# A gated linear attention with an MoE behind it, one core: transposes of k ahead of the products, all products of a chunk in one piece, and the first tile in four parts

## The chip, the cores and the metric

The kernel runs on one core of one Trainium2 chip. The metric is the device time of one execution in microseconds; 715.45 us is the median of three runs of the kernel before (712.55 to 721.03).

## The reference

For 4 batches x 8 heads, a sequence of 768 steps with head size 48 goes through a complex diagonal recurrence; the result goes through a gated two-layer product (384 to 2048 to 384).

```python
mag = np.sqrt(a_re * a_re + a_im * a_im)
scale = np.minimum(mag, 0.999) / (mag + 1e-06)
a_re_n, a_im_n = (a_re * scale, a_im * scale)
for t in range(S):
    ar, ai = (a_re_n[:, :, t, :, None], a_im_n[:, :, t, :, None])
    new_re = ar * S_re - ai * S_im
    new_im = ar * S_im + ai * S_re
    kv = np.einsum('bhd,bhe->bhde', k[:, :, t], v[:, :, t])
    S_re, S_im = (new_re + kv, new_im)
    y[:, :, t] = np.einsum('bhd,bhde->bhe', q[:, :, t], S_re)
...
h = x @ w_in
g = h * np.clip(h + 3.0, 0.0, 6.0) / 6.0
return (g @ w_out).astype(np.float32)
```

## The kernel before

The sequence is cut into 24 chunks of 128 steps (6 for each batch; the chunks of two batches alternate, so chunk `cc` hands its state to chunk `cc+2`). Three chunks make a tile of `a` (`z`, 8 tiles, two in memory at a time) and also a group of MoE (8 groups of 384 rows). The work is written as thirteen generators, called streams. One string, `ORDER`, names the stream whose next step is issued; a step runs to the next `yield`. Nothing is reordered afterwards: each engine, and SyncE (SP) with its DMAs, takes its instructions in the order in which the steps were issued and waits in that order. Some letters of the string:

- `Z` (`load`, line 344): a DMA of one part of a tile of `a`. `PARTS` (line 79) cuts a tile in two, one for each half `f` of the steps, 9 rows each.
- `N`, `O` (`normal`, line 361): the parts with even and with odd number are brought to the reference's magnitude, in four steps: Square on ScalarE (ACT, line 373), a product on POOL, or on VectorE (DVE) for tile 0 (376), Ln and Exp (377, 381, 382), a product (383), then three or four DVE products (385 to 393). Two buffers `sq` serve all parts.
- `C` (`chain`, line 398): cumulative products over the 64 steps of a half: seven steps of four DVE operations (408 to 410), four smaller ones, and a last step (437 to 451) that multiplies all 18 rows at once, six DVE operations of 882 elements with a temporary `fx`. Then POOL works out the decay of the state between chunks (455 to 475) and six DMAs lay it out as `cw` (482).
- `P`, `Q` (`prep`, line 493; `Q` is chunk 1 alone): q and k of a chunk, multiplied with the chain's result, and laid out by six DMAs as `kq` (543); one DMA brings `vt` (551).
- `A` (`mat`, line 556), the attention of one chunk on TensorE (PE): scores `pA` from `kq`, masked by DVE into `am` (570); products of v into `py` (578 to 597); if there is a chunk behind it, k is transposed into `pt` and copied by ACT to `kn`, which takes `am`'s buffer (599 to 604); if there is one before it, the state decays (POOL 612, DVE 618) and its products are added into `py` (620 to 627); `pG` updates the state (632 to 639); ACT and DVE split `py` into `xh` and `xl` for MoE (647, 648). The PSUM pool `ps_a` has three buffers for `pA`, `py`, `pt` and `pG`.
- `M` (`moe`, line 652): for each of 16 blocks `f` of the hidden size nine products into `ph` (690), the gate (ACT 696, DVE 699 or 708, called `hs` below), and the products of the block before into `po` (673 to 677). Groups 0 to 2 have three `po` products for a block, groups 3 to 7 nine.
- `D`, `W` load and convert the 16 weight blocks (DVE 308, 312, ACT 307, 316, POOL 317); `G` and `S` look at the weights' ranges and split them; `V` ends it.

```python
        py = ps_a.tile([C, 3, C], F32, tag="ps", name="py")
...
        if has_g:
            kn = pe_.tile([C, NH, L], F32, tag="am", name="kn", bufs=1)
```

Of the kernel before, what the change touches and what calls it, by code (L numbers as in the profile page):

```python
# [35 lines left out]
ORDER = (
    "ZNNZZZONQNOOOCNCCCCOCCCCCCOCCPDWPODDDWPQPPPPPPWWQWQWDQQQQPOANAPPWDAAACDWAAWWAAWNWNWPDDDWWPZPCWWCNAZA"
    "APDDWCWAAADACOAAACAACCACAMMCWMMMDCMMMMMCCCMMMWPMMMMMMMMMMMMPWPPMMMMMMMMWMDMMCMMWPPWMMMMMOWWPPMMMMMMM"
    "NMMMMOMWWMMMMDMMMAMMAMMPPMMMMANAAAPWPPMMPWNWMMMOPPPAAMMMMMMMMMMMMACPCMMMPGCPCGPGGGCCCCCMCMMMMMMMMPAA"
    "MGGZZCCCPAAAACOMMMMMMMMPPPMAAAMMMMMPPNAAAPPAPAAANMONAAPOMPMNMMMMMMOPMAAPMGMMMMMCMMMMPMMGPMMGGAAAACCC"  # L40
    "MMCPCMMMMMCCCGAMMMGMMMMPPPPGGAPPPMSSCAMMMMMMMAMMAMMMMGMMMMCCPCMGMAAPAAMMPPPPMMMMMMGMAMGMMMPMZZAAMMMM"
    "MMCNNPPAMAMMOMNMMAPOPMPMMMMMOMNOAMAMMMMMMPMMMMGMMMMMMMMMMAGAPCMMMMMPPCPAAAMMACMMMAACAACCCCMMGPMMMMMA"
    "MMPPPMMGGPGAMPPCCCMMMMMMMMMMMZAMAMASSCCNMMMMMMGNMMMPSMMPPSMMAPMMMMMPMASMSMMZGNSMPMMMMPPMMOMNAMSSMMMM"
    "MMPAASSSAOPMMMMMMAASPMMMMMPPMSAPAAAGPPPPPSMMMOMMOCMMMMMMMMMACCMMSSSSAMMMSSSMMMMMMCMPPMMMMGMCAMMPCPSG"
    "GAPMMCAMAMMAMMMZCPMCMMMMMCCPPPAAAMAACNNMMMMMMMMSMMMMMMMAAMMMMMMCCMMMMZPAMMMMMMMMMMMAMMMMAMMMMAMSPPMP"
    "MPOMMMSAAAMMMMPMPMMSMMMCMMMMMMMMOMMMMMMMMPPOANAMMSSMMMMMMMPMMPPMPPAOAAMMMAMSMMMMMMMMMAMNMMMMMPPMMMCA"
    "MPCMMMMAAACCMMMMMMMMMMMPMMMAPAAMMMMMMPMMMAMMMMCMMMMMMMMMMMMZCMMMMMMMMPCMCMNPCCMMMMMMMNMMAAAAMMMMAMPC"
    "MMMMMMZMAAAAMNCMCMMMPMMMMAMAPMMMMMMMCMPMMMMPPPPMMMMMAMMMMMMMMMMMMMMNOMOMMMPMMMMMAPAPMMMMMMMMAMMAMMMM"
    "MOMAMMPAMPAOPPPPPMMMMMMMMMAMMMMCCMMMMMPCCMMMMMMMAMAAMMMMMMMMMMMPPCMMMMMPPMMMMACAAAMMMCMMMMMCMAMMMMMM"
    "PMMMCCAAMAMCMMMMMMMMMGMAMMMPMAAACACPCMAPAMMMMPMMMMMMMMPPMPPMMMMMMMMMMMMMMMMMMMMMPAPMMMMMMMMAAMPPMMMM"  # L50
    "MMMMMMMMMMMMMAAMAMAMMMMMPMPPPMMMMMMMMMMMMMMMMMMMMMMMMMMMAMAPPPMMMMMMMMMMMMPMMMMMMMMMMMMMMMMPAAMMPMPM"
    "MAMMMMMMMMMMMMMMMPMMAAAMMMMMMMMMPAAAMMMMMMMMMMMMMMMMMAAMMMAAMMMMMMMMMMMMMMMMMMMMMMMMMMMMMMMMMMMMMMMM"
    "MMMMMMMMMMMMMMMMMMMMMVMMMMMMMMMMMMMMMMMMMMMMMMMMMMMMMMMMMMMMMMMMMMMMMMMMMMMMMMMMMMMMMMMMMMMMMMMMMVMM"
    "MM"
)
# [175 lines left out]
def tile_gated_attention_moe(ctx, tc, aL, GL, vL, wL, maskL, qkvaL, out):  # L231
    nc = tc.nc
    V, A, P, T, SP = nc.vector, nc.scalar, nc.gpsimd, nc.tensor, nc.sync
# [322 lines left out]
    def mat(cc):  # L556
        g, c = GROUP[cc]
        while cc not in KQ:
            yield "wait"
# [37 lines left out]
        yield
        if has_g:
            kn = pe_.tile([C, NH, L], F32, tag="am", name="kn", bufs=1)
            for hf in range(2):  # L600
                pt = ps_a.tile([C, 4, L], F32, tag="ps", name="pt")
                for i in range(4):
                    T.transpose(pt[:, i], kt[:, hf * 4 + i], ident[:L, :L])
                A.activation(kn[:, hf * 4 : hf * 4 + 4], pt, AF.Copy)  # L604
                if hf and not has_s:
                    free("kq")
                yield
        if has_s:
            q, c2 = CHUNK[cc]
            while q not in CWs:  # L610
# [1 line left out]
            P.tensor_tensor(
                state2,
                state2,
                CWs[q][:, :, :, c2].rearrange("p h k -> p k h").unsqueeze(3).to_broadcast([L, 2, NH, 64]),
                ALU.mult,
            )
            V.tensor_tensor(xs, xs, xj, ALU.add)
            yield
        if has_s:  # L620
# [287 lines left out]
```

## Time and profile before

| | us |
|---|---|
| runs of the kernel before | 712.55, 715.45, 721.03 |
| the profiled execution | 718.27 |
| its span, from the first to the last instruction | 716.5 |
| PE busy, DVE busy, ACT busy, POOL busy in the span | 593.6, 510.7, 352.5, 175.9 |
| mean granted clock of PE | 0.975 of full speed |

A row of a timeline gives start and length in us, engine, line of the kernel, operation, written tile <- read tiles, shape and count; what stands in brackets is the engine's idle time before it and what ended that. A row of SPq is a DMA's issue on SyncE's queue, not its transfer. A shape is partitions x elements of one partition.

### The profile page before, as it was taken

The page shows a single profiled execution, that of the slowest core. Times are in us where ns is not written, and L with a number is a line of the kernel's source. Part 1 is how long each engine was busy: PE and PEld are TensorE (multiplying, and loading weights), DVE is VectorE, ACT ScalarE, POOL GpSimd, SP SyncE. Part 2 cuts the span into 40 slices and gives each one's busy share as a digit, 9 for nine tenths or more (in the row PEclk, how much of TensorE's full clock was granted, in tenths as well). Part 3 has the DMA queues.
Part 4 walks back from the last instruction along what each step waited for, and adds up shares of the span by engine and source line. Part 5 has one row for each costly group of instructions (what it writes and reads, how often), then busy time and mean ns, then how long its engine had stood idle before and what let it go on. Part 6 is the DMA issues. An engine that isn't in the chain of part 4 may idle for free.

```text
span 716.5 us, 12111 instructions
## 1 busy us (share of the span) xinstructions
PE 593.6 (83%) x4433; PEld 521.7 (73%) x4433; DVE 510.7 (71%) x995; ACT 352.5 (49%) x721; POOL 175.9 (25%) x193
## 2 busy tenths in 40 slices
PE   0005359998568989989998999999999999999995
PEld 0004347776356767777777999999999998998995
DVE  3998857989858876787888657987688855453432
ACT  5334332565657776567646454444643443423332
POOL 0204230342143143315740333221302211300000
PEclk9999999999689999999999999999999999999998
DMA  9009872257746885476566234242453244140001
GB/s 344 23 18 206 253 211 78 67 121 163 183 102 161 194 225 96 127 179 157 104 126 150 80 72 79 86 70 90 82 126 45 82 82 78 50 60 34 1 0 38
DMA packets 55508, 79.61 MB, mean 111 GB/s; under 512 B 12432, under 2 KB 40208, under 8 KB 55440
## 3 DMA queue, kind: packets, MB, share of 16 engines
q1 hardware_dynamic: 55440, 78.75, 46.7%
q8 instruction: 37, 0.61, 0.4%
q14 instruction: 31, 0.25, 0.1%
HBM read 51.05 MB, written 4.72 MB: 78 GB/s over the span
## 4 chain that ended last, share of the span: by engine, by line
PE 38%; DMA 9%; DVE 8%; ACT 7%; issue 3%; POOL 3%; SPq 1%; ACTq 0%; DVEq 0%; POOLq 0%
PE ph L690 15%; PE po L673 5%; PE po L674 5%; PE po L675 5%; DMA kq<-gg 3%; PE py L585 3%; DMA out_dram<-ot 2%; DMA wgs<-in_wL_dram 2%; PE pA L569 2%; PE po L677 2%; PE pG L632 1%; ACT r L696 1%; DVE gg L528 1%; POOL gg L518 1%; DVE pr L408 1%
## 5 line engine op out<-in xcount | busy, mean ns | idle before, releaser
L696 ACT ACTIVATE r<-ph,half 128x384 f32<-128x384 f32 x128 | 73.7, 577 | 113.9 <-PE ph L690 109.4
L677 PE MATMUL po<-wo,hs 128*128 128x384 f32 x288 | 108.3, 509 | 16.7 <-DVE hs L708 16.7
L690 PE MATMUL ph<-xh,win_l 128*128 128x384 f32 x384 | 102.7, 376 | 2.8 <-ACT xh L647 2.8
L569 PE MATMUL pA<-kq 96*128 96x128 f32 x384 | 53.9, 296 | 61.2 <-DMA kq<-gg 59.3
L569 PEld LDWEIGHTS pA<-kq 96*128 96x128 f32 x384 | 51.7, 209 | 63.8 <-issue 61.4
L690 PE MATMUL ph<-xl,win_h 128*128 128x384 f32 x384 | 90.5, 344 | 1.0 <-DVE xl L648 1.0
L690 PE MATMUL ph<-xh,win_h 128*128 128x384 f32 x384 | 89.9, 342 | 0.0
L699 DVE SCALAR_TENSOR_TENSOR ph<-r,ph 128x384 f32<-128x384 f32 x80 | 44.8, 560 | 62.5 <-ACT r L696 62.3
L673 PE MATMUL po<-wh,gl 128*128 128x384 f32 x240 | 84.9, 354 | 4.2 <-DVE gl L704 3.8
L677 PEld LDWEIGHTS po<-wo,hs 128*128 128x128 f32 x288 | 53.9, 197 | 44.6 <-DVE hs L708 18.5
L674 PE MATMUL po<-wout_l,gh 128*128 128x384 f32 x240 | 81.9, 341 | 0.0
L675 PE MATMUL po<-wh,gh 128*128 128x384 f32 x240 | 81.0, 337 | 0.0
L690 PEld LDWEIGHTS ph<-xh,win_l 128*128 128x128 f32 x384 | 70.4, 192 | 14.4 <-ACT xh L647 2.9
L704 DVE TENSOR_TENSOR gl<-ph,gh 128x384 fp32r<-128x384 f32 x80 | 44.5, 557 | 41.0 <-ACT gh L702 40.9
L690 PEld LDWEIGHTS ph<-xl,win_h 128*128 128x128 f32 x384 | 69.4, 191 | 1.9 <-DVE xl L648 1.5
L690 PEld LDWEIGHTS ph<-xh,win_h 128*128 128x128 f32 x384 | 69.5, 190 | 0.6 <-issue 0.6
L702 ACT ACTIVATE gh<-ph 128x384 fp32r<-128x384 f32 x80 | 39.2, 490 | 60.9 <-DVE ph L699 60.9
L408 DVE TENSOR_TENSOR pr<-z 128x288 f32<-128x288 f32 (+2 forms) x176 | 66.6, 419 | 1.4
L518 POOL TENSOR_TENSOR gg<-gg,u 128x384 f32<-128x384 f32 x18 | 19.5, 1084 | 142.4 <-ACT u L516 126.7
L632 PE MATMUL pG<-vt,kn 128*96 128x64 f32 x320 | 34.9, 268 | 21.4 <-ACT kn L604 21.4
L673 PEld LDWEIGHTS po<-wh,gl 128*128 128x128 f32 x240 | 45.5, 189 | 8.4 <-DVE gl L704 7.3
L632 PEld LDWEIGHTS pG<-vt,kn 128*96 128x96 f32 x320 | 33.3, 183 | 24.6 <-ACT kn L604 22.1
(101 smaller groups left out, 1042.9 us busy)
## 6 DMA issues: line engine op xcount, KB each, us to landing
kq<-gg SPq DMA_DIRECT2D x138, 128.0 KB, 4.7
ws<-in_wL_dram SPq DMA_DIRECT2D x16, 768.0 KB, 7.2
wgs<-in_wL_dram SPq DMA_DIRECT2D x32, 384.0 KB, 3.8
z<-in_aL_dram SPq DMA_DIRECT2D x16, 612.0 KB, 5.5
vt<-in_vL_dram SPq DMA_DIRECT2D x24, 256.0 KB, 5.2
out_dram<-ot SPq DMA_DIRECT2D x24, 192.0 KB, 1.9
u<-in_GL_dram SPq DMA_DIRECT2D x23, 192.0 KB, 5.0
gg<-in_GL_dram SPq DMA_DIRECT2D x23, 192.0 KB, 2.6
```

The source lines that it names most:

```text
L408: V.tensor_tensor(pr[:, j], src, fac[:, j : j + 1].to_broadcast([C, *shape]), ALU.mult)
L569: T.matmul(pA[:, i], kt[:, hf * 4 + i], qt[:, hf * 4 + i], start=True, stop=True)
L632: T.matmul(pG[:, n], kn[:, n], vt[:, n], start=True, stop=True)
L673: T.matmul(po[i], gl[:, ts], wout_h[f], start=f == 0, stop=False)
L674: T.matmul(po[i], gh[:, ts], LATE["wl"][:, f], start=False, stop=False)
L675: T.matmul(po[i], gh[:, ts], wout_h[f], start=False, stop=f == NFF - 1)
L677: T.matmul(po[i], hs[0][:, ts], wout[f], start=f == 0, stop=f == NFF - 1)
L690: T.matmul(ph, w[:, f, kt * C : (kt + 1) * C], xx[:, kt], start=k == 0, stop=k == 8)
L696: A.activation(r, ph, AF.Relu, scale=1.0 / 6.0, bias=half)
L699: V.scalar_tensor_tensor(ph, r, 1.0, ph, ALU.min, ALU.mult)
L702: A.activation(gh, ph, AF.Copy)
L704: V.tensor_tensor(gl, ph, gh, ALU.subtract)
```

## The change

1. In `mat` the transposes of k into `pt` and the copy to `kn` stand right behind the scores, and the decay of the state behind them. All products into `py`, those of v and those of the state, are issued in one step after that. A chunk with a chunk before it takes one step of `A` less (196 steps become 176).
2. `kn` is now `kk`, with a buffer of its own.
3. The last step of `chain` goes by 9 rows in place of 18: twelve operations of 441 elements in place of six of 882 (112 steps of `C` become 136); `fx` shrinks with it.
4. Tile 0 of `a` is cut in four parts (5 and 4 rows for each half); the other tiles stay at two.
5. `ORDER` is another one throughout. The first two hundred letters or so and the stretch around chain 2 are shown.

```diff
-    GS=3, VTB=2, IL=2
+    GS=3, VTB=2, IL=2, R0=5
...
-    "ZNNZZZONQNOOOCNCCCCOCCCCCCOCCPDWPODDDWPQPPPPPPWWQWQWDQQQQPOANAPPWDAAACDWAAWWAAWNWNWPDDDWWPZPCWWCNAZA"
-    "APDDWCWAAADACOAAAACAACCACAMMCWMMMDCMMMMMCCCMMMWPMMMMMMMMMMMMPWPPMMMMMMMMWMDMMCMMWPPWMMMMMOWWPPMMMMMMM"
-    "NMMMMOMWWMMMMDMMMAMMAMMPPMMMMANAAAPWPPMMPWNWMMMOPPPAAMMMMMMMMMMMMACPCMMMPGCPCGPGGGCCCCCMCMMMMMMMMPAA"
-    "MGGZZCCCPAAAACOMMMMMMMMPPPMAAAMMMMMPPNAAAPPAPAAANMONAAPOMPMNMMMMMMOPMAAPMGMMMMMCMMMMPMMGPMMGGAAAACCC"
...
+    "ZZNNOZZZNDNONQDDOONOZNNDOOOCCCCCOCCCCCCCCCCCWPPCPQPPPPPPWQWOQNQDQQWWAANPNWPWAAAPWDQAAPWWZNWOWOAZOAPC"
+    "CDDDWCWCCWCNAAPDDPPWAAAADAAACAWCAWAACWCWMMMMMMMMCCWCMMMMWMMMMCMWCWMCMMMMPPDMMMMMMMDMPDPPWPPMCMMMMMMM"
+    "MWWPNMMMMDMWWWMMMMMMMMMMMMAAMPNAAAPMMPPNMMMMWMMMPPMMMMMOAPOMMWMMPMMOAAAMMMMCPCPMCMMGMMMMCMMGAGCPACGP"
+    "CCAMMMGCPACCCCCCCMGGMMMMMMMZMPPMZMMAAAPMMMMPMPPNMMMNPONAAAPAAOPPMPMNAAAPOMMMMMMOMMMMMAGGGPCCPPCCMMMM"
...
 PARTS = [
-    [(f, x, min(9, 3 * n - x)) for f in range(2) for x in range(0, 3 * n, 9)] for _, n, _ in CHAINS
+    [(f, x, min(r, 3 * n - x)) for f in range(2) for x in range(0, 3 * n, r)]
+    for t, n, _ in CHAINS
+    for r in [9 if t else R0]
 ]
...
-        for x in range(0, w, 18):
-            xn = min(18, w - x)
+        for x in range(0, w, 9):
+            xn = min(9, w - x)
...
-        while cc not in VT:
-            yield "wait"
-        vt = VT.pop(cc)
-
-        py = ps_a.tile([C, 3, C], F32, tag="ps", name="py")
...
-        for n in range(NH):
-            ymm(n, False, vt, am[:, n], n < 4, False)
-        for k in range(2):
-            for n in range(k, NH, 2):
-                ymm(n, True, vt, am[:, n], False, k == 1 and not has_s)
-        if not has_g:
-            free("vt")
-        yield
         if has_g:
-            kn = pe_.tile([C, NH, L], F32, tag="am", name="kn", bufs=1)
+            kn = pe_.tile([C, NH, L], F32, tag="kk", name="kk", bufs=1)
...
             V.tensor_tensor(xs, xs, xj, ALU.add)
             yield
+        while cc not in VT:
+            yield "wait"
+        vt = VT.pop(cc)
+
+        py = ps_a.tile([C, 3, C], F32, tag="ps", name="py")
...
+        for n in range(NH):
+            ymm(n, False, vt, am[:, n], n < 4, False)
+        for k in range(2):
+            for n in range(k, NH, 2):
+                ymm(n, True, vt, am[:, n], False, k == 1 and not has_s)
+        if not has_g:
+            free("vt")
         if has_s:
-            sp = xs
             for n in range(NH):
-                ymm(n, False, sp, qt[:, n], False, False)
+                ymm(n, False, xs, qt[:, n], False, False)
             for k in range(2):
                 for n in range(k, NH, 2):
-                    ymm(n, True, sp, qt[:, n], False, k == 1)
+                    ymm(n, True, xs, qt[:, n], False, k == 1)
             free("kq")
-            yield
+        yield
```

## Rows read from the trace of the kernel before

**Rows 1.** Windows by stage: stretch, its length, busy us and instructions, PE clock, DMA.

```profile
0.00:117.61 117.61, 36.01 (x260) 30.67 (x261) 88.75 (x175) 45.83 (x78) 25.77 (x36) 1.00 0.57 163
117.61:221.24 103.63, 83.13 (x559) 64.64 (x559) 84.90 (x151) 56.73 (x117) 31.14 (x34) 0.90 0.56 132
221.24:716.50 495.26, 474.44 (x3617) 426.38 (x3615) 337.00 (x670) 249.97 (x527) 118.99 (x124) 0.98 0.43 95
...
5.60:20.34 14.74, 0.00 (x0) 0.00 (x0) 8.68 (x12) 9.53 (x16) 1.00 (x1) 1.00 0.93 368
...
167.90:186.06 18.16, 8.68 (x46) 7.00 (x44) 16.69 (x55) 12.27 (x31) 0.93 (x4) 0.80 0.65 173
...
176.70:186.70 10.00, 0.03 (x1) 0.04 (x1) 8.74 (x33) 6.99 (x17) 1.23 (x7) 0.60 0.72 170
186.70:218.00 31.30, 22.93 (x220) 16.86 (x220) 19.27 (x25) 18.02 (x38) 11.02 (x9) 0.80 0.61 137
...
396.00:702.00 306.00, 301.61 (x2362) 289.64 (x2361) 194.90 (x381) 129.50 (x262) 56.93 (x64) 1.00 0.31 64
```

(The busy times stand in the order PE, PE's weight loads, DVE, ACT, POOL.)

**Rows 2.** Waits of PE, 0 to 108 us and 108 to 216: total, times, longest.

```profile
PE pA L569 <- DMA kq<-gg: 59.3, 1, 59.3
PE pG L632 <- ACT kn L604: 18.6, 1, 18.6
...
PE po L677 <- DVE hs L708: 12.3, 4, 10.1
PE py L585 <- DVE am L570: 5.4, 1, 5.4
```

**Rows 3.** Timeline of the first tile and the start of chain 0.

```profile
5.61 1.16 ACT L373 ACTIVATE sq<-z 128x1152 f32<-128x1152 f32 x1 [3.59 <-DMA z<-in_aL_dram]
...
19.34 2.21 POOL L376 TENSOR_TENSOR sq<-sq 128x576 f32<-128x576 f32 x1 [18.35 <-ACT sq L373]
20.34 1.90 DVE L408 TENSOR_TENSOR pr<-z 128x288 f32<-128x288 f32 x2
...
22.27 0.31 DVE L409 TENSOR_TENSOR z<-pr 128x144 f32<-128x144 f32 x1
...
23.59 1.40 POOL L376 TENSOR_TENSOR sq<-sq 128x576 f32<-128x576 f32 x1 [2.03 <-ACT sq L373]
23.70 1.45 DVE L409 TENSOR_TENSOR z<-pr 128x144 f32<-128x144 f32 x1
```

**Rows 4.** Groups by line and shape: count, busy us, mean ns, idle before.

```profile
L373 ACT ACTIVATE sq<-z 128x1152 f32<-128x1152 f32 x16 | 18.5, 1158 | 11.3 <-DMA z<-in_aL_dram 11.3
...
L386 ACT ACTIVATE sq<-sq 128x576 f32<-128x576 f32 x16 | 10.8, 678 | 12.1 <-DVE sq L385 12.0
...
L449 DVE TENSOR_TENSOR z<-z,fx 128x882 f32<-128x882 f32 x8 | 8.6, 1073 | 0.0
```

**Rows 5.** Timeline from the end of chain 0 to cw0's issue.

```profile
42.35 1.07 DVE L449 TENSOR_TENSOR z<-z,fx 128x882 f32<-128x882 f32 x1
...
50.62 3.92 SPq L543 DMA_DIRECT2D kq<-gg  x6
...
64.10 0.54 POOL L455 COPY pps<-z 128x18 f32<-128x18 f32 x1
...
67.81 4.12 SPq L482 DMA_DIRECT2D cw<-ww  x6
```

**Rows 6.** Timeline around chunk 1's pG and the start of MoE.

```profile
93.49 1.16 ACT L373 ACTIVATE sq<-z 128x1152 f32<-128x1152 f32 x1 [4.45 <-DMA z<-in_aL_dram]
...
97.45 2.82 PE L632 MATMUL pG<-vt,kn 128*96 128x64 f32 x16 [18.62 <-ACT kn L604]
...
112.34 1.31 PE L690 MATMUL ph<-xh,win_l 128*128 128x384 f32 x3
```

**Rows 7.** PE's timeline where both halves of py stand together.

```profile
635.72 1.08 PE L585 MATMUL py<-am,vt 128*32 128x128 f32 x32
...
637.61 0.79 PE L690 MATMUL ph<-xh,win_h 128*128 128x384 f32 x3
```

More of the change, by code (lines that the diff above doesn't have):

```diff
@@ L32 @@
     PV=2, SZ='33333333', CS='3.3.3.3.3.3.3.3', GGB=1, SQB=2, ZB=2, XB=2, WTB=4, LAG=1, RB=2, OV=1, KQB=2,
-    GS=3, VTB=2, IL=2
+    GS=3, VTB=2, IL=2, R0=5
 )
 ORDER = (
-    "ZNNZZZONQNOOOCNCCCCOCCCCCCOCCPDWPODDDWPQPPPPPPWWQWQWDQQQQPOANAPPWDAAACDWAAWWAAWNWNWPDDDWWPZPCWWCNAZA"
-    "APDDWCWAAADACOAAACAACCACAMMCWMMMDCMMMMMCCCMMMWPMMMMMMMMMMMMPWPPMMMMMMMMWMDMMCMMWPPWMMMMMOWWPPMMMMMMM"
-    "NMMMMOMWWMMMMDMMMAMMAMMPPMMMMANAAAPWPPMMPWNWMMMOPPPAAMMMMMMMMMMMMACPCMMMPGCPCGPGGGCCCCCMCMMMMMMMMPAA"
-    "MGGZZCCCPAAAACOMMMMMMMMPPPMAAAMMMMMPPNAAAPPAPAAANMONAAPOMPMNMMMMMMOPMAAPMGMMMMMCMMMMPMMGPMMGGAAAACCC"
@@ L41 @@
[L41 to L54, printed above, removed]
+    "ZZNNOZZZNDNONQDDOONOZNNDOOOCCCCCOCCCCCCCCCCCWPPCPQPPPPPPWQWOQNQDQQWWAANPNWPWAAAPWDQAAPWWZNWOWOAZOAPC"
+    "CDDDWCWCCWCNAAPDDPPWAAAADAAACAWCAWAACWCWMMMMMMMMCCWCMMMMWMMMMCMWCWMCMMMMPPDMMMMMMMDMPDPPWPPMCMMMMMMM"
@@ new lines @@
+    "MWWPNMMMMDMWWWMMMMMMMMMMMMAAMPNAAAPMMPPNMMMMWMMMPPMMMMMOAPOMMWMMPMMOAAAMMMMCPCPMCMMGMMMMCMMGAGCPACGP"
+    "CCAMMMGCPACCCCCCCMGGMMMMMMMZMPPMZMMAAAPMMMMPMPPNMMMNPONAAAPAAOPPMPMNAAAPOMMMMMMOMMMMMAGGGPCCPPCCMMMM"
+    "MAMAMMMMMMCCCCAGACMMMMMMMMMMPGGPMMMMPPPAMGGMAPPPCASAMMMMMMMMMMMMAMMGSGCCCAMMMMMMPMMGCCCAMMCMMPAMMGMM"
+    "MMMMMMCMMMPZZAPPPNPPPAPAPMNNNAMMMMMMMMMMOAMAAAMMPMOPMMMAGOAMMPMMOMMMMMMMMMMCMPMMGMAMMCMAAPMMMMCAACCC"
+    "AGGCMMMPMPMPMMMCAPAAPAAMMMMAPMMCGPPCMMMMMMMGGMACCCZMPPMMNMCCMMMMSPZCMMNMMMMMMMMMMMMPPMNSPPGPMMSMAMMA"
@@ new lines @@
+    "MMMMMMPPPPMMMSSSSSNMMMSAMMSOMMAPMMMMPPPASAGPSMMMMMMMPASSAOOAMOSMCMMMMMMCCMMMPPCMPMMMMMMPSMMCMGMMMMMM"
+    "PAPACGGMCCCMMCMMMMMMMZAMMAMMSAMMMCCMAANCMMMMMMAMMMMMPMMMMPACMMZMMMCCMSMMMMMSMMCMMMMMCPMMPPMMSMMAPAAM"
+    "MMMMSOPPPPMMMPPAAOMMMMMMMMAMSSMMMMAMMNMMMNSANSAAAMMMPMMMSOAPPAAMMMMMMMPSSSSMMMMMMMMMMPMOMMMMMMMMMMCC"
+    "AMPMPPPMMMMMMMMMMMAAACMMPCMPMMMMMMMMMMMMPMAAMAMMMMMMMCMMMZMMMCMMCMMMMMMMMMAACZMMMCMMMMMMCAMMPPMMMCCM"
+    "MMMCMMCMMMMMMMCAANAPCMMMMMMMMMMPMPMMMMMMMMMMMMAMAAAPCMOOMPMPMMMMMAPPPMMMPMMMMMMNMMMOMMMMMMMNOMMMAMPM"
@@ new lines @@
+    "MMAMMAMMMMAMMAAMNAMMMMMMMPPMMMPMAMMMMMMMMMMCCMMMCMMMMMMPPPPPMACMAAMMAMMMMMMMMMMAPMCMMMAPAMPPMMMMPMMM"
+    "MMMAMMMMCCCMCMMCMCAAMMMMMMMMMMMMAMCMMCCCMMMMMMMMMMMPMMPMCAAAAMMMCPMMMMMMMMMPPPPAMMMPMMMMMMPMMPMMMMMM"
+    "MMMMMMMAAMAAPAAMAMMMMMPPPMPMMMMMMMMAMMMMMMPPPMMMMMMMMMAMMMMMMMAAAMPMMMMAMMMMMMPPPPMAMMMMMMMMMMMPMMMM"
+    "MMMMMMMMMMMMMMMMGMMMMMMMMMMMMMMMMMPMMMMMMMMMAMMMMMMMMMMMMMMMMMMMMMMAAMMMMMAAMMMAMMMMMMMMMMMMMMMMMMMM"
+    "MMMMMMMMMMMMMMMMMMMMMMMMMMMMMMMMMMMMMMMMMMMMMMMMMMMMMMMMMMMMMVMMMMMMMMMMMMMMMMMMMMMMMMMMMMMMMMMMMMMM"
@@ L55 @@
+    "MMMMMMMMMMMMMMMV"
 )
@@ L65 @@
 NG, NCH = len(SIZES), B * S // C
+R0 = int(PAR["R0"])
 IL, SEQ = int(PAR["IL"]), S // C
@@ L573, in mat @@
             yield
+        if has_g:
+            kn = pe_.tile([C, NH, L], F32, tag="kk", name="kk", bufs=1)
+            for hf in range(2):
+                pt = ps_a.tile([C, 4, L], F32, tag="ps", name="pt")
+                for i in range(4):
+                    T.transpose(pt[:, i], kt[:, hf * 4 + i], ident[:L, :L])
+                A.activation(kn[:, hf * 4 : hf * 4 + 4], pt, AF.Copy)
+                if hf and not has_s:
+                    free("kq")
+                yield
+        if has_s:
+            q, c2 = CHUNK[cc]
+            while q not in CWs:
+                yield "wait"
+            P.tensor_tensor(
+                state2,
+                state2,
+                CWs[q][:, :, :, c2].rearrange("p h k -> p k h").unsqueeze(3).to_broadcast([L, 2, NH, 64]),
+                ALU.mult,
+            )
+            V.tensor_tensor(xs, xs, xj, ALU.add)
+            yield
         while cc not in VT:
@@ L596, in mat @@
             free("vt")
-        yield
-        if has_g:
-            kn = pe_.tile([C, NH, L], F32, tag="am", name="kn", bufs=1)
[L600 to L606, printed above, removed]
-                yield
-        if has_s:
-            q, c2 = CHUNK[cc]
-            while q not in CWs:
-                yield "wait"
[L612 to L620, printed above, removed]
-            sp = xs
+        if has_s:
             for n in range(NH):
-                ymm(n, False, sp, qt[:, n], False, False)
+                ymm(n, False, xs, qt[:, n], False, False)
             for k in range(2):
                 for n in range(k, NH, 2):
-                    ymm(n, True, sp, qt[:, n], False, k == 1)
+                    ymm(n, True, xs, qt[:, n], False, k == 1)
             free("kq")
-            yield
+        yield
         if has_g:
```

## The prediction

> **What bounds the kernel now.** I read the stages first [rows 1], then the waits of TensorE (PE) [rows 2], and then the timelines of the places where it waits. The span falls into three parts, cut at the VectorE (DVE) product that closes the first step of MoE group 0 (117.61 us) and of group 1 (221.24 us). In the first part PE works 36.0 of 117.6 us and waits 59.3 us for the first kq and 18.6 us for one kn copy [rows 2]. DVE works 88.8 of it. In the second part DVE works 84.9 of 103.6 us and PE 83.1 at a mean granted clock of 0.90: neither is full, and they hold each other up. In the third PE works 474.4 of 495.3 us, 301.6 of 306.0 in the late stage [rows 1]: there only less PE work helps. So the change can win in DVE's long start and in group 0; behind that there is little to give back.
>
> The profiled execution took 718.27 us (span 716.5 and 1.8 around it), 2.8 over the median of 715.45. I sum against 718.27 and take 2.8 off at the end.
>
> **How I read the order.** Each letter issues one step of a stream, and every engine takes its instructions in that order, so the two order strings give what stands ahead of what in each queue. I wrote both out. Up to the first product of group 0, DVE gets the same work in both, but for one small step: ten weight blocks, three prep chunks, tiles 0 and 1 normalised, chain 0, and chain 1 up to its last step. Hence the 88.8 us stay, and a gain there must come out of DVE's 28.9 us of idle time.
>
> **First tile in four parts.** In the old start the first z lands at 5.61 and the chain begins at 20.34 [rows 3]; in these 14.74 us ACT works 9.53 and DVE 8.68 [rows 1], in turns. A Square of 1152 elements takes 1158 ns, a Copy of 576 takes 678 [rows 4]: 0.83 ns per element and 0.20 us fixed. Halving five ACT operations of each of two parts adds 10 x 0.20, and four accumulator reads, taken at 0.20 too, are added: 2.8 us more ACT work. Against it the first piece is 5/9 of a part (128 x 2 x 9 x 68 numbers of 4 bytes, at the 368 GB/s of that stage 1.7 us) and lands some 0.7 us earlier, and two pieces in flight fill some of the turns; only two sq buffers exist, so the third waits for the first. Bounds: -1.5 (the turns close) to +2.1 (2.8 - 0.7, nothing closes). Stepping the four pieces through both queues I end at about 20.9: I take +0.5.
>
> **Tile 1 moved behind chain 0.** Beside chain 0 POOL now runs three products over tile 1. Where one runs, a DVE product with two SBUF inputs stands still: a subtraction that takes 0.31 us at 22.27 takes 1.45 at 23.70, ending with POOL's 1.40; the pair at 20.34 takes 1.90 under POOL's 2.21 [rows 3]. Each costs about 1.1 us. In the new order one of the three is issued there; two are past chain 0: -2.2 for the first scores. The Trainium skill has this rule (GPSIMD Engine Reference, Specifications): GpSimd's SBUF interfaces are shared with VectorE, with contention where a DVE instruction has two SBUF inputs. The trace agrees (1.45 for 0.31). By that rule the 2.2 us are only postponed, since the moved products meet DVE's prep and chain 1 instead; by the row alone I could have kept them as a gain to the end. I keep them out of the sum to M's start: 0, bounds -2.2 and +1.
>
> **Last step by 9 rows.** Six operations of 882 elements, 1.07 us each [rows 4], become twelve of 441. Half the length costs between half the time (0) and half plus about 0.1 us fixed each (+0.6 per chain). The nearer row is the 882 one, hardly above its streaming time; I take +0.4 per chain, where DVE is short, three chains: +1.2. In the PE-filled part five more chains cost nothing: DVE works 194.9 of 306 us [rows 1]; if that cover went, 2 us.
>
> **cw0 ahead of kq0 on SP.** Chain 0 ended at 43.42 and kq0 was issued from 50.62, 7.2 us later [rows 5]. The new order puts cw0's six DMAs first: POOL's work for them to their issue took 3.7 us (64.10 to 67.81), and the issue 4.12: 7.8 us after the chain. So kq0 is 0.6 late; its transfer stands behind 1536 runs of 12 bytes (six times 16 x 8 x 2) and may lose as much again as their issue takes. I take +0.6, bounds 0 and +4.7. Everything behind kq0 on SP (vt0, u2, kq1) shifts with it.
>
> **From the first scores to M's start.** kn no longer takes am's buffer, so the transposes need not wait for the products of v. But no PE wait in this trace is for that buffer; the 18.6 us before 97.45 end with the ACT copy of kn1, which stood in ACT's queue behind a Square waiting 4.45 us for tile 2's z (93.49) [rows 6]. In the new order z2 is issued right behind the state exchange of chunk 0, before kq2, by the DVE work ahead of it about 12 us earlier, but kn1 stands behind both Squares of tile 2 and behind weight blocks 6 and 7. I walk it: chain 0 ends at 43.4 + 0.5 - 2.2 + 0.4 = 42.1, kq0 is issued 7.8 later and lands 8.7 after its first issue, as now (50.62 to 59.3, [rows 2, 5]), so first pA at 58.6 and am0 done by 63. From there to block 6 DVE has 27.7 us ahead (mean durations of the line groups: prep 2 4.4, the rest of tile 1 6.5, blocks 2 to 6 9.9, attention 2.6, three chain steps 4.3): 90.5. Behind it on ACT come win_h, block 7, Square, POOL's 1.4 us and Ln, 5.5 in all: kn1 at 96, pG1 from 96 to 99 (from 97.45 now). Then the one new wait: the products of v into py2 now stand behind the state's decay, with pG2 and M queued behind them; their 32 products cost about 1 us there. M starts at about 112, as now (112.34). Sum up to there with the terms above: 0. Bounds -6 (a third of the 17.2 us closes that DVE idles between 20.34 and 117.61: 28.9 less 5.6 before the first z and 6.1 of rows 1's 14.74) and +8 (below).
>
> **Group 0.** Now DVE runs 18 us of chain 2 and prep 5 without a product for MoE (167.90 to 186.06, 16.7 us of work [rows 1]), and PE waits for that product for 10.1 us [rows 2]; the granted clock is 0.60 there and 0.80 in the 31 us after [rows 1], that is, much of both at the lower of the two levels. The new order cuts this stretch by products of MoE into pieces of about 7, 10 and 11 us of DVE work, with 3.5 us of PE work (nine ph and three po groups) or more between. PE then waits about 6 us in the second, 4 in the third and again some 5 for am5: 15 where it waited 17.7 (12.3 + 5.4, [rows 2]): -2.7. DVE is idle 12.0 of the 31.3 us after 186.70 [rows 1], partly for POOL's product over tile 3, whose ACT input now comes before two of the three ot copies: -1.8. Together -4.5; the +1.2 of the half steps is in my walk. Bounds: -18.7 (all DVE idle of the second part) and +3.
>
> The Trainium skill has a rule that bears on the clock (TensorE: Matmul & The Clock Gate, What's actually happening): the array's clock is halved when idle and released by activity. The trace agrees (0.60 where PE idled for 10 us). By it three waits instead of one bring no clock back, and the sum has no term for it; without it I would add the lost share of these stages, some -5.
>
> **py at once.** In the late stage 32 products of v cost 1.01 us alone; where both halves already stand together they take 1.89 (635.72 to 637.61) [rows 7] for 2.02. Twenty chunks have both, about 16 of them where PE is full: 16 x 0.13 = -2.0, bounds 0 and -2.6. The transposes cost the same at either place. The wait on the state is covered by MoE steps between.
>
> **Sum.** 0 - 4.5 - 2.0 = -6.5: 711.8, and less 2.8: **709.0**.
>
> **Rivals.**
> - *Group 0 closes up* (PE's waits there are mostly covered and the clock stays high): some 11 of the 18.7 us and the 2 of py, -13, so 702.5. For: DVE idle of 18.7 us and PE idle of 20.5 there. Against: DVE's pieces are still longer than PE's.
> - *Nothing that counts moves*: PE's work and DVE's 88.8 us are the same and the transposes never waited; 715. For: 474.4 of 495.3. Against: the 10.1 us wait is plainly one of order.
> - *Slower: kn1 late on ACT.* Place: the queue ahead of kn1 (both z2 Squares, blocks 6 and 7, whose loads now follow kq2's first half). If they hold ACT 8 us past the walk, on a load as it stood at 93.49, or by a late kq0, kn1 comes near 104, M at 120: +8, the 2 of py off, group 0 gaining nothing: 718.3 + 6 - 2.8 = 721.5. It decides from kn1 at about 101 on, where the gain of group 0 is spent. For: it is what happened at 93.49. Against: z2 is issued earlier.
>
> **Chances.** Forecast 0.50 (own range 704 to 714), group 0 closes 0.18, nothing 0.14, slower 0.18. About 1%, 7 us, can be told from no change: faster is below 708.3. The forecast gives 0.23 to faster and 0.27 to same; the closing 0.18 to faster; nothing 0.12 same, 0.02 slower; the slow one 0.16 slower, 0.02 same. Rounded: 0.41, 0.41, 0.18. The range takes in the rivals and half of the bounds of group 0: 697 to 724.
>
> **What would show it.** First pA between 58 and 61; kn1's copy at 94 to 98; M's start within 4 us of 112; no PE wait of 10 us in group 0, but two or three of 4 to 6; group 1's first product near 215 to 217; the late stage shorter by 2. I am wrong if M starts past 116 or before 107, or if the part behind group 1's start differs by over 5 us.

## The result and the profile after

The kernel after takes 708.52 us (median of five runs, 704.94 to 710.02) where the kernel before took 716.28 on the same chip: ratio 0.9885, 95% interval 0.9846 to 0.9923. Run once more among the experiments it gave 703.85 against 717.31, 0.982 [0.9772, 0.9868]. So it is faster by 1.2 to 1.8%; the forecast was 709.0. The profiled execution took 704.94 us, 13.3 less than that of before. Where these 13.3 us lie, by the windows cut as in [rows 1], at the first product of group 0 (110.77, before 117.61) and of group 1 (210.30, before 221.24):

```profile
0.00:110.77 110.77, 31.24 (x266) 28.20 (x266) 93.56 (x196) 47.61 (x93) 27.52 (x36) 1.00 0.61 176
110.77:210.30 99.53, 84.38 (x548) 65.50 (x549) 81.44 (x160) 57.33 (x118) 32.10 (x35) 0.88 0.60 137
210.30:703.10 492.80, 470.21 (x3621) 427.95 (x3619) 340.74 (x699) 247.78 (x525) 118.34 (x123) 0.99 0.43 94
```

The start is 6.8 us shorter, group 0 is 4.1 shorter (99.5 for 103.6) and the rest 2.5 (492.8 for 495.3). DVE works 4.8 us more in the start (93.56 for 88.75), yet it ends earlier: DVE's idle time there fell from 28.9 to 17.2 us.

PE's waits from 0 to 108 us and from 108 to 216, against [rows 2]:

```profile
PE pA L572 <- DMA kq<-gg: 57.6, 1, 57.6
PE pG L633 <- ACT kk L583: 9.9, 2, 8.4
PE pt L582 <- DVE am L573: 9.1, 1, 9.1
...
PE po L678 <- DVE hs L709: 11.9, 5, 4.7
PE pt L582 <- DVE am L573: 4.3, 1, 4.3
```

The wait of 18.6 us for the copy of k is now 9.1 for the mask (the transposes come first, and the second `pt` needs a buffer of `ps_a` that the mask frees) and 8.4 for the copy: much the same time before the state, split in two. The longest wait for a product of DVE is 4.7 us in place of 10.1; the sum of these waits is 11.9 us for 12.3.

The timeline of the first tile, of chain 0's last step and of the issues behind it, against [rows 3, 5]:

```profile
21.19 2.03 DVE L411 TENSOR_TENSOR pr<-z 128x288 f32<-128x288 f32 x2
21.20 1.70 POOL L379 TENSOR_TENSOR sq<-sq 128x576 f32<-128x576 f32 x1 [20.20 <-DVE z L393]
...
35.81 0.62 DVE L448 TENSOR_TENSOR fx<-z 128x441 f32<-128x441 f32 x1
35.84 0.65 POOL L458 COPY pps<-z 128x18 f32<-128x18 f32 x1 [12.93 <-DVE z L413]
...
39.41 3.90 SPq L485 DMA_DIRECT2D cw<-ww  x6
...
49.04 3.79 SPq L546 DMA_DIRECT2D kq<-gg  x6
```

Chain 0 starts 0.85 us later (21.19 for 20.34) and meets one POOL product in place of three that cost it something: the two of [rows 3], and in the trace of before

```profile
26.83 2.01 DVE L408 TENSOR_TENSOR pr<-z 128x288 f32<-128x288 f32 x2
```

Its last step takes 7.10 us (35.81 to 42.91), 6.26 before. POOL's work for cw0 starts at 35.84, with that step and not behind it: its input is there before the last step runs. So cw0's issue is over 5.7 us before kq0's begins.

And from z2's load to the start of MoE, against [rows 6]:

```profile
71.57 0.94 SPq L360 DMA_DIRECT2D z<-in_aL_dram  x2
...
92.77 0.85 ACT L583 ACTIVATE kk<-pt 128x384 f32<-128x384 f32 x2
...
93.30 2.82 PE L633 MATMUL pG<-vt,kk 128*96 128x64 f32 x16 [8.38 <-ACT kk L583]
...
96.33 0.68 DVE L638 COPY state<-pG 96x512 f32<-96x512 f32 x1
...
103.33 1.57 PE L633 MATMUL pG<-vt,kk 128*96 128x64 f32 x16
105.48 0.79 PE L691 MATMUL ph<-xh,win_l 128*128 128x384 f32 x3 [0.58 <-ACT xh L648]
```

MoE starts at 105.48 (before 112.34). The state's copy at 96.33 starts only 0.2 us after the product is through (93.30 + 2.82 is 96.12), but the copy stood in DVE's order behind weight block 7 (counted from 0), which ended at 96.4: both come together.

The products into py, by groups, over the whole span:

```profile
L610 PE MATMUL py<-am,vt 128*32 128x128 f32 x768 | 28.5, 294 | 0.0
L610 PE MATMUL py<-kq,state 96*32 96x128 f32 x640 | 22.5, 283 | 3.3 <-DVE state L597 3.3
```

In the trace of before the same two groups took 31.2 and 22.6 us, with 7.3 us of waits ahead of v's products and 0.8 ahead of the state's.

### The profile page after: what moved, and what is told of

The parts are those of the page before. It is cut to its first block, busy times and chain, and to the rows that moved or that the text cites. A ratio compares the mean times of both kernels' runs of the same rounds, so it can differ in the third digit from the quotient of the medians.

```text
span 703.1 us, 12198 instructions
## 1 busy us (share of the span) xinstructions
PE 585.8 (83%) x4433; PEld 521.6 (74%) x4433; DVE 515.7 (73%) x1054; ACT 352.7 (50%) x735; POOL 178.0 (25%) x193
## 4 chain that ended last, share of the span: by engine, by line
PE 30%; DVE 17%; ACT 10%; DMA 9%; issue 6%; POOL 5%; SPq 3%; DVEq 0%; ACTq 0%; POOLq 0%
PE ph L691 12%; PE po L674 4%; PE po L675 3%; PE po L676 3%; DVE pr L411 3%; DMA kq<-gg 3%; PE po L678 3%; DMA wgs<-in_wL_dram 2%; DVE gg L531 2%; PE py L610 2%; DVE ph L700 2%; ACT r L697 2%; POOL gg L521 2%; PE pG L633 2%; ACT gh L703 2%
## 5 line engine op out<-in xcount | busy, mean ns | idle before, releaser
L678 PE MATMUL po<-wo,hs 128*128 128x384 f32 x288 | 108.2, 512 | 17.2 <-DVE hs L709 17.1
L572 PE MATMUL pA<-kq 96*128 96x128 f32 x384 | 56.4, 302 | 58.6 <-DMA kq<-gg 57.6
L691 PE MATMUL ph<-xh,win_l 128*128 128x384 f32 x384 | 100.9, 371 | 0.6 <-ACT xh L648 0.6
L572 PEld LDWEIGHTS pA<-kq 96*128 96x128 f32 x384 | 53.9, 215 | 60.6 <-issue 57.6
L411 DVE TENSOR_TENSOR pr<-z 128x288 f32<-128x288 f32 (+2 forms) x176 | 65.1, 411 | 1.3
L531 DVE TENSOR_TENSOR gg<-u,z 128x384 f32<-128x384 f32 x92 | 49.1, 590 | 0.4
L379 POOL TENSOR_TENSOR sq<-sq 128x576 f32<-128x576 f32 x14 | 23.3, 1665 | 95.2 <-ACT sq L376 74.8
```

What stands on the lines that cost most here:

```text
L411: V.tensor_tensor(pr[:, j], src, fac[:, j : j + 1].to_broadcast([C, *shape]), ALU.mult)
L531: V.tensor_tensor(gg[:, k, :, 1 - i].rearrange("p d (f s) -> p f d s", f=2), u[:, 2 * i : 2 * i + 2], zv[:, k], ALU.mult,)
L678: T.matmul(po[i], hs[0][:, ts], wout[f], start=f == 0, stop=f == NFF - 1)
L691: T.matmul(ph, w[:, f, kt * C : (kt + 1) * C], xx[:, kt], start=k == 0, stop=k == 8)
```

## The experiments

Times are medians with the ratio to the kernel before on the same chip. Runs 1 to 4 stood beside each other, 5 to 8, and 9 to 11. Between kernels that did not, a ratio is good to some 0.6%, as the two results of the kernel after show.

**1. The kernel after again.** No edit; the base for runs 2 to 4.

> The changed kernel again, as the yardstick of the runs beside it. Both theories: about 708.5 us, 1.1% under the kernel before; M's start near 105.5, first product of group 1 near 210.

703.85 us, ratio 0.982. Group 1's first product at 210.37.

**2 and 3. The code without the order, and the order without the code.** The first takes the new code with the old string, its letters mapped step by step (against the kernel after):

```diff
-    GS=3, VTB=2, IL=2, R0=5
+    GS=3, VTB=2, IL=2, R0=9
...
-    "ZZNNOZZZNDNONQDDOONOZNNDOOOCC
+    "ZNNZZZONQNOOOCNCCCCOCCCCCCOCC
...
```

The second takes the old code with the new string, v's products at the letter of the first transposes (against the kernel before; the first tile stays in two parts and the last step at 18 rows):

```diff
-    "ZNNZZZONQNOOOCNCCCCOCCCCCCOCC
+    "ZZNNZODNQNDDOOZDOCC
...
```

> Code of the change (transposes first, products together, kk, 9 rows; first tile in two parts) with the order of before, letter by letter: each chain's three last letters doubled, the step of v's products dropped where it joins the state's. Theory 'order': the new order makes the gain; this runs as before or a little over it, 714 to 719, because the half steps cost DVE 0.84 us per chain (7.10 for 6.26) and only the late stage wins 2 by the joined products. M starts near 112. Theory 'code': transposes and their buffer make the gain, 706 to 711 with M's start near 106.

> Code of before (products of v apart, kn in am's buffer, 18 rows, first tile in two parts) with the order of the change; v's products are issued with the first transposes. Theory 'order': as the changed kernel or up to 3 us under it, since DVE is spared the half steps: 704 to 710, M's start 103 to 106. Theory 'code': the copy to kn now waits for the products that read am, and the gain falls away: 714 to 719.

The code alone: 724.24 us, 1.0092 [1.0058, 1.0127]. The order alone: 749.44, 1.0465 [1.0414, 1.0517]. Either half of the change is slower than the kernel before, and slower than any of the four theories had it. The order alone has all the gain up to group 1 (its first product at 210.18) and loses some 42 us against the kernel after behind it. PE's waits say where; of the code with the old order:

```profile
PE po L678 <- DVE hs L709: 24.4, 10, 11.3
PE pG L633 <- ACT kk L583: 21.3, 2, 18.2
```

and of the new order with the old code:

```profile
PE py L585 <- DVE am L570: 38.2, 23, 10.0
```

The new string puts little between the scores and the step behind them. With the old code that step holds v's products, which need the mask; PE, which takes its work in order, stands 38 us for DVE, with MoE's products behind. Of the code's loss with the old order a part may be the 9 rows, which alone cost 0.6% (run 9).

**4. The first tile in two parts.** The kernel after with the old cut of tile 0.

```diff
-    GS=3, VTB=2, IL=2, R0=5
+    GS=3, VTB=2, IL=2, R0=9
...
-    "ZZNNOZZZNDNONQDDOONOZNNDOOOCC
+    "ZZNNZODNQNDDOOZDOCC
```

> The changed kernel with the first tile in two parts. If the four parts cost what the start of chain 0 shows (21.19 us for 20.34), 0.9 us less at M's start and as much or nothing at the end: 707 to 709. If the early landing helps more than that shows, 1 to 2 us more than the changed kernel.

706.4 us, 0.9828 [0.9782, 0.9875], beside 0.982 for four parts. Group 1's first product came 1.6 us earlier (208.74), but the groups' outputs, from the second to the sixth, go out within 0.7 us of each other (in runs 4 and 1 at 286.52 and 286.78, and at 508.64 and 508.00). Four parts bring nothing that lasts, and cost nothing.

**5. Tile 2's loads late again.** z2's two loads go back behind kq2's first half and three weight blocks, its second Square back behind them on ACT.

```diff
-WNWOWOAZOAPCCDDDWCWCCWCN
+WNWOWOAAPCCDDDZZWCWCCOWCN
```

> The changed kernel with the two loads of tile 2's z moved back behind kq2's first half and three weight blocks on SP, and the second of its Squares moved behind block 6 on ACT. Theory 'z2': M starts early because z2 is there when ACT comes to it; here ACT and then DVE wait for it as in the kernel before, M's first gate product comes at 114 to 118 and the time is 3 to 7 us over the changed kernel's. Theory 'queue': M's start follows from the work ahead on DVE and z2 lands in time anyway: within 1.5 us of the changed kernel.

713.74 us, 0.9939 [0.9899, 0.9978]: some 4 to 9 us over the kernel after. Around chunk 1's pG:

```profile
95.97 0.85 ACT L583 ACTIVATE kk<-pt 128x384 f32<-128x384 f32 x2
96.50 2.82 PE L633 MATMUL pG<-vt,kk 128*96 128x64 f32 x16 [11.96 <-ACT kk L583]
99.36 0.69 DVE L638 COPY state<-pG 96x512 f32<-96x512 f32 x1 [2.28 <-PE pG L633]
```

Here the copy of k is late on ACT, and DVE waits 2.28 us for the product behind it. MoE starts 3.3 us later (108.81; first gate product 114.10, as theory 'z2' had it), group 1 by 4.0 (214.29). So the early load is worth about half of the 6.9 us.

**6. Chunk 1's transposes right behind its scores.** Aimed at the 8.4 us wait.

```diff
-ZOAPCCDDDWCWCCWCNAAPDD
+ZOAAAPCCDDDWCWCCWCNPDD
```

> The changed kernel with chunk 1's two transposes and their copies issued right behind its scores, ahead of tile 2's Squares and weight blocks 6 and 7 on ACT. Theory of the prediction (kn1 on ACT gates M's start): PE's 8.4 us wait for the copy goes, pG1 comes 8 us earlier and M's start 3 us or more. Theory 'queue': DVE takes the state's update in its own order and is busy without a gap until then, so M's start stays within 1 us and the time within 1.5.

708.68 us, 0.988 [0.9792, 0.9968].

```profile
83.53 0.85 ACT L583 ACTIVATE kk<-pt 128x384 f32<-128x384 f32 x2
...
96.38 0.68 DVE L638 COPY state<-pG 96x512 f32<-96x512 f32 x1
97.12 2.08 PE L572 MATMUL pA<-kq 96*128 96x128 f32 x8 [5.78 <-DVE state L638]
```

The copy of k comes 9.2 us earlier and the wait is gone, but the state's copy stays at 96.38 (96.33), since its place in DVE's order is the same, and MoE starts at 105.35. The largest wait of PE in that stretch costs nothing; PE stands as long elsewhere.

**7 and 8. Where v's products stand.** The kernel after, with v's products in a step of their own place, ahead of the transposes or right behind them; kk keeps its buffer.

```diff
+        def of_v():
+            vt = kit["vt"] = VT.pop(cc)
+            kit["py"] = ps_a.tile([C, 3, C], F32, tag="ps", name="py")
+            for n in range(NH):
+                ymm(n, False, vt, am[:, n], n < 4, False)
...
             kn = pe_.tile([C, NH, L], F32, tag="kk", name="kk", bufs=1)
+            of_v()
```

(In the second, the call stands behind the copy of the second `pt`.)

> The changed kernel with the products of v issued ahead of the transposes, where a kn in am's buffer would force them; kk keeps its own buffer, 9 rows and the split tile stay. Theory 'mask': PE then stands behind DVE's mask in each chunk, as it did by 38 us in all with the old code in the new order, and the time is 735 to 748. Theory 'buffer': those 38 us were for the shared buffer or the six-fold half steps; with kk apart the time stays within 3 us of the changed kernel's.

> The changed kernel with the products of v issued right behind the transposes, apart from the state's. By the term 'py at once' of the prediction it loses the 0.13 us of each of 16 chunks, 2 us; by the mask theory a little more, where DVE's second mask is later than the two transposes: 2 to 8 us over the changed kernel. If together or apart does not matter: within 1.5 us.

Ahead: 748.61 us, 1.0453 [1.0381, 1.0524], the loss of run 3, with the same wait:

```profile
PE py L584 <- DVE am L573: 38.2, 22, 9.8
```

So it isn't the shared buffer of am and kn that costs, but that v's products come before the mask is done. Right behind the transposes: 725.47 us, 1.011 [1.0038, 1.0181], 16 to 21 us over the kernel after where at most 8 were expected. Its span is 21.3 us longer. PE's waits sum up to some 7 us more (7.7 us for the mask and 2.6 for the copy of k ahead of py where there were none, 7.9 for the state in place of 3.3, and some others less; v's products don't read the copy, so that wait is for a buffer of `ps_a`), and PE is busy for 13.8 us more (599.6 for 585.8) with the same products. One place in the PE-filled stage shows how:

```profile
452.31 1.93 PE L584 MATMUL py<-kq,state 96*32 96x128 f32 x32 [3.17 <-DVE state L624]
454.18 2.82 PE L638 MATMUL pG<-vt,kk 128*96 128x64 f32 x16
...
457.55 0.52 PE L681 MATMUL po<-wh,gh 128*128 128x384 f32 x1
...
458.69 0.34 PE L679 MATMUL po<-wh,gl 128*128 128x384 f32 x1
```

Behind a wait of 3.17 us the state's products take 1.93 us (1.06 in the kernel after), pG 2.82 (1.57) and a po product 0.52 (0.34) until 458.5. That is 0.87 + 1.25, and another 0.9 by which the six po products from 456.76 to 458.50 stand further apart than the 0.18 us behind them: 3.0 us, so this wait costs about twice its length. The window from 450 to 460 us has a granted clock of 0.66 there; in the kernel after every window of 10 us from 310 to 680 us gives 1.00. Not all of the 13.8 us is of this kind. Behind group 1's start PE is busy for 11.6 us more (470.21 in the kernel after):

```profile
209.17:724.40 515.23, 481.78 (x3622) 431.92 (x3621) 345.93 (x699) 247.92 (x525) 117.12 (x123) 0.97 0.42 90
```

The clock records of this trace give 23.8 us at the lower level between 211 and 700 us, those of the kernel after 10.2; products at half speed for 13.6 us more would make up to 6.8 of the 11.6 (an estimate). The rest stays open. The two halves of py have 3.2 us of the 13.8 (54.2 for 51.0), part of it at the lower level.

Nor does every such wait cost double. Two of run 7:

```profile
332.26 2.20 PE L682 MATMUL po<-wo,hs 128*128 128x384 f32 x6 [2.98 <-DVE hs L713]
...
465.00 1.08 PE L584 MATMUL py<-kq,state 96*32 96x128 f32 x32 [3.17 <-DVE state L623]
```

Behind the first the six po products run at about full speed (2.20 us; the six of the next block, at 335.88, take 2.10). Behind the second the state's products still take 1.08, and some 4 us run slower after them (pG 2.00 for 1.57, po 0.52 for 0.34).

**9. The last step by 9 rows alone**, in the kernel before.

```diff
-        for x in range(0, w, 18):
-            xn = min(18, w - x)
+        for x in range(0, w, 9):
+            xn = 9
```

> The kernel before with only the last step of the chains by 9 rows, at the same three letters. Theory 'price': chain 0's last step took 7.10 us after and 6.26 before; with three chains where DVE is short the first product of group 1 comes 2.5 us later (723.7 in place of 221.24 is not meant: 221.24 becomes 223.7 in the trace), and the ratio is about 1.003. Theory 'spacing': the shorter operations let MoE products in sooner; first product of group 1 not later than 221.5, ratio 0.997 to 1.000. The last steps of all eight chains together: +6.7 us of DVE work by the first, which PE-filled stages should hide.

721.08 us, 1.006 [1.0015, 1.0105]. Neither theory fits: group 1's first product came at 216.20, early as 'spacing' had it, but the time is longer, as 'price' had it or more. The last step again took 7.1 us. By itself the edit is no gain. It loses behind group 1's start, in the profiled execution 500.8 us for 495.3, PE busy for 3.0 us more and idle for 2.5 more, though the order there is the same; why stays open.

**10 to 12. Chunk 5 earlier**, tries at a faster kernel: run 10 moves the attention of chunk 5 ahead of tile 3 and prep 6, run 11 also the last gates of group 0 ahead of chain 2's end, run 12 mends run 10's order on SP and ACT. The stretches of the string, in this order:

```diff
-MMMPMPPNMMMNPONAAAPAAOPPMPMNAAAPOM
+MMMAAPMAPPAANMMMNPMMAAAONPOPPPNPOM
...
-CPACGPCCAMMMGCPACCCCCCCMGGMMMMMMMZMPPMZMMAAAPMMM
+CPAMMCGPCCAMGCPAMMMMMMCCCCMMMMMMMCCCGGZPPZAAAPMM
...
-MMMPMPPNMMMNPONAAAPAAOPPMPMNAAAPOMMMMMMOM
+MMMAAPMAPPAAPPNMMMNPPMMAPAAONONMMMMMPOMOM
```

> The kernel after, with the attention of chunk 5 (scores, mask, transposes, decay, products) issued ahead of the normalisation of tile 3 and of most of prep 6; nothing else moved. In the kernel after, PE waits 4.34 us at 198.15 for the mask of chunk 5, which stands in DVE's queue behind prep 6 (idle 3.75 and 1.30 us there), and its state waits for POOL's products over tile 3. Theory 'order of the queues gates group 1': its first product comes at 203 to 206 in place of 210.3, and the time falls by 4 to 6 us (ratio 0.977 to 0.981 where the kernel after gives 0.982 to 0.9885). Theory 'work postponed': group 1 starts early, but tile 3 and prep 6 are late, and by the sixth output the gain is under 1.5 us.

> The same, and in addition the gate products of group 0's blocks 13, 14 and 15 issued ahead of the last steps of chain 2 (in the kernel after PE waits 4.71 us at 175.60 for block 13's, ready to run since 167.4, behind eight steps of DVE work). Theory 'PE's waits in group 0': 3 to 5 us less than the run with chunk 5 early alone. Theory 'DVE bound': chain 2 ends 2 us later, group 1 starts at the same time as in that run within 1 us, and the times agree within 1.5 us.

> The kernel after with the attention of chunk 5 early, as in the run before, but with the six DMAs of kq6, vt6 and the loads of prep 7 left ahead of chunk 5's state exchange on SP, and the first gate of group 1 ahead of prep 7 on ACT. In the run before, kq6 was issued at 204.43 in place of 195.02, behind the exchange; the gate vectors of prep 7 came 8 us later, and ACT waited 6.48 us for them with group 1's first gate behind (217.20 in place of 210.30). Theory 'one queue': with SP's order kept, group 1's first product comes at 202 to 206 and the time is 3 to 6 us under the kernel after (ratio 0.974 to 0.984). Theory 'work postponed': the first product comes as early, but prep 6 and tile 3 come late, PE waits for their chunks, and the ratio stays at 0.983 to 0.990.

715.75 us (0.9985 [0.9944, 1.0027]), 717.0 (1.0 [0.9957, 1.0044]) and 711.29 (0.9894 [0.9854, 0.9935]): none is better than the kernel after. In run 10 group 1's first MoE products (`ph`) do start earlier (202.15 for 205.87), and then:

```profile
204.43 3.83 SPq L546 DMA_DIRECT2D kq<-gg  x6
...
213.01 0.52 ACT L519 ACTIVATE gg<-z 128x384 f32<-128x384 f32 x1 [6.48 <-DMA kq<-gg]
...
217.20 0.56 DVE L709 SCALAR_TENSOR_TENSOR hs<-r,ph 128x384 f32<-128x384 f32 x1 [8.05 <-ACT r L697]
```

kq6 was issued at 195.02 in the kernel after; now it stands on SP behind chunk 5's state exchange. The vectors of prep 7 wait for its buffer, ACT waits for them, and group 1's gate stands behind on ACT: 217.20 for 210.30, so neither theory of run 10 had the first product right. Run 12 puts SP's order right, and PE then waits 4.57 us for chunk 5's `xh`, which stands on ACT behind the work of tile 3 and the outputs: first product at 212.02. So both theories of that run fell at their first step, the early start, though the ratio is in the range of 'work postponed'. Run 11's earlier gates took nothing off run 10's time (717.0 and 715.75), as 'DVE bound' had it, though group 1 started 2.3 us earlier (214.86), which it had not.

## Why the prediction was right, and where it was not

The time (709.0 for 708.52) is right, and the term that carried most of the forecast, group 0, came out near its size, though not by its parts. But a term set at zero is the largest of all: against the profiled execution, for which the sum was made, it is -13.3 and not -6.5 (704.94 where 711.8 was forecast). That the median of that measurement agrees to half a microsecond is luck in part: the profiled execution of the kernel before is 2.8 us over its median as the forecast had it, that of the kernel after is the fastest of its five and 3.6 under, and the second measurement, 703.85, is 5 us under the forecast.

| step | forecast | measured in the trace |
|---|---|---|
| first tile in four parts | +0.5 | +0.85; nothing at the end (run 4) |
| 9 rows, per chain | +0.4, at most +0.6 | +0.84 |
| cw0 ahead of kq0 | +0.6 | 0 |
| first scores | 58.6 | 57.63 |
| copy of chunk 1's k | 96 | 92.77 |
| start of MoE against before | 0 (-6 to +8) | -6.9 |
| group 0 | -4.5 | -4.1 |
| py at once, late stage | -2.0 | not told apart; the stage behind group 1's start is 2.5 shorter |

*Start to MoE: the term that was mis-sized.* The step that failed is the walk that had "kn1 at 96" and MoE "at about 112, as now". It was too long before the copy and behind it. The copy came at 92.77, 3.2 us ahead of the walk: the first scores were 1.0 earlier, DVE took 26.4 us from am0 to block 6 and not 27.7 (62.12 to 88.53), and ACT came to the copy 4.2 us behind block 6 and not 5.5. Both Squares of tile 2 stand ahead of the copy as walked, but with z2 issued at 71.57 they ran at 78.86 and 89.34 without a wait; undoing that (run 5) brings the copy to 95.97 and takes 3.3 us back. From pG to MoE the walk kept 16 us, the 14.9 of before and a wait; it took 12.2 (93.30 to 105.48). There the walk took the copy of k as the gate. Run 6 moves it by 9 us for nothing: in the kernel after DVE's own queue is the gate, and what was won is DVE's idle time, 11.7 us less of it. I had bounded that gain at 6, a third of the 17.2 us of idle time between chain 0's start and MoE's first gate product, and given it no weight; 6.0 us of the 17.2 are left. "Before 107" was named as what would prove me wrong, and it did.

Of the last stretch, from the state's copy to MoE (9.15 us, before 12.03), 2.1 us look like the clock's: pG2 takes 1.57 us and the state's products 1.08, in the trace of before 2.82 and 1.93. Run 10 speaks against that. Its order is the same up to there, chunk 2's products ran at the lower level, and MoE starts 0.06 us later than in the kernel after (its first gate product, 111.57, comes 0.8 later):

```profile
102.27 1.93 PE L610 MATMUL py<-kq,state 96*32 96x128 f32 x32
...
104.33 0.57 ACT L319 ACTIVATE win_h<-ws 128x384 fp32r<-128x384 f32 x1 [2.35 <-DVE ws L315]
...
105.54 0.77 PE L691 MATMUL ph<-xh,win_l 128*128 128x384 f32 x3
```

The `xh` that MoE needs stands on ACT behind this conversion of a weight block (`win_h`, at 104.49 in the kernel after), and ACT waits for DVE there: DVE's queue once more. What made the other half of the 6.9 us, beside z2, no run shows.

*cw0.* I let POOL start behind the chain's end, as if its input were the last step's result; the trace has it start with the last step (35.84). The bound of 0 was the right value: kq0 was issued 6.1 us behind the chain (49.04), where 7.8 was forecast and 7.2 was before.

*9 rows.* 441 elements take 0.62 us against 1.07 for 882: 0.08 above the half, and twelve times that is 1.0, of which 0.84 show. Six more fixed parts was the right count, but 0.1 us was too little for each: by 144 elements in 0.31 us and 882 in 1.07 [rows 3, 4] it is 0.16, so 1.0 per chain. It is part of DVE's 4.8 us of added work in the start, which the closed idle time outweighs.

*Tile 1 behind chain 0.* One collision at 21.20 in place of those of [rows 3]: chain 0 ends at 42.91 though it began 0.85 later and is 0.84 longer, which is the 2.2 us forecast. That they would be only postponed came true as well: behind chain 0 a DVE operation took 1.68 us (at 52.21) beside POOL's 1.41, for 0.56 else, and a pair 2.05 (at 90.69) beside POOL's 1.40, for 0.82; these too are in the 4.8 us.

*Group 0.* The size is near, the parts are not. PE's waits of 4.71, 1.58 and 4.34 us are where I had 6, 4 and 5, none of 10; but two more, of 2.36 and 2.60, stand at the stage's start, and all sum to 16.2 us where they were 17.7: -1.5 for the -2.7 forecast. DVE's idle time in the stage is 18.1 us for 18.7: -0.6 for -1.8. What fell most is DVE's busy time, by 3.5 us (81.44 for 84.90), though its last steps are longer. In the trace of before a pair of prep's products stands beside two operations of POOL:

```profile
204.30 1.39 POOL L376 TENSOR_TENSOR sq<-sq 128x576 f32<-128x576 f32 x1 [1.21 <-ACT sq L373]
204.31 4.00 DVE L528 TENSOR_TENSOR gg<-u,z 128x384 f32<-128x384 f32 x2
205.66 2.24 POOL L612 TENSOR_TENSOR state<-state,cw 96x1024 f32<-96x1024 f32 x1
...
209.44 1.01 DVE L528 TENSOR_TENSOR gg<-u,z 128x384 f32<-128x384 f32 x2
```

It takes 4.00 us where the next pair takes 1.01; in the kernel after all sixteen of these products take 0.55 to 0.56 each. So by DVE's account most of the 4.1 us is less standing beside POOL in this stage, for which the forecast had no term. No run tests that, and that -4.1 is near -4.5 is in part luck.

The Trainium skill's rule that idling lowers the array's clock (TensorE: Matmul & The Clock Gate, What's actually happening) was taken to bring nothing back there, and the granted clock of the stage is 0.88 (0.90 before): the trace agrees. Group 1's first product came at 210.30 and not 215, because MoE started 6.9 us early.

*py at once.* The two groups take 51.0 us for 53.8 over all chunks, but 2.7 of the 2.8 lie before group 1's start, mostly in v's products (9.1 us for 11.6), more of which ran at the higher level there (0.27 us each, 0.42 at the lower). Behind it, where the term was forecast, they are busy for 36.9 us and were for 37.0. Busy time can't show the term, since it doesn't tell how closely the groups follow each other; the places do:

```profile
463.01 1.08 PE L610 MATMUL py<-am,vt 128*32 128x128 f32 x32
463.90 1.06 PE L610 MATMUL py<-kq,state 96*32 96x128 f32 x32
464.89 0.45 PE L674 MATMUL po<-wh,gl 128*128 128x384 f32 x1
```

Both take 1.88 us to the next product here; in the trace of before each took 1.01 by itself (404.13 to 405.14, 416.45 to 417.46). So the price of 0.13 per chunk holds, and with it the sum of 2 us for 16 chunks. That the stage is 2.5 us shorter doesn't show it: run 1's trace of the same kernel has it 1.9 shorter still (490.9). Run 2 has the joined products too and is slower than before, so they aren't what the change lives on.

What I had not seen is that parts 1 and 5 depend on each other. I wrote that "no PE wait in this trace is for that buffer" and priced the new place of v's products at the 2 us of py. True for the old string; but the new string leaves so little PE work behind the scores that, with v's products in their old place, PE stands 38 us for the mask (runs 3 and 7), and even right behind the transposes the kernel is 16 to 21 us slower (run 8). The code part is the condition for the order, and the order is the gain.

Of the rivals, "group 0 closes up" did not happen (PE's waits there sum to 16.2 us where they were 17.7), though the second time, 703.85, is near its 702.5 for another reason. "Nothing that counts moves" fell with all three stages. "kn1 late on ACT" is what run 5 makes of the kernel in small. Why the medians stand 7.8 and 13.5 us under the kernel before in two measurements of one kernel stays open.

## What to carry to other kernels

Where engines take their work in a written order, price an order and the code it was written for together: run each half alone before crediting either. A wait on the busiest engine is worth something only if nothing else gates the same point; look for the engine whose queue reaches that point last (here DVE's copy at 96.33), and sum its idle time, for that is what a new order can give. In a stage filled by PE a wait of some 3 us can cost twice its length, as in run 8; look at the products behind it before counting so, for behind another they ran on at full speed (run 7).
